# Keys and values of linear attention packed in 64-row halves: the summary product on four array quarters

## The chip, the cores and the metric

The kernel runs on one core of one Trainium2 chip. What counts is the device time of one execution in microseconds. The core has a matrix engine (TensorE, in the profile PE, with its weight loads as a row of their own, PEld), a vector engine (VectorE, DVE), an activation engine (ScalarE, ACT), GpSimd (POOL) and the engine SyncE (SP), which here only issues DMAs.

## The reference, cut to what matters

```python
def _attn_ref(q, k, v):                      # 8 batches, 8 heads, 576 positions, 64 wide
    q_s = np.exp(q - np.max(q, axis=-1, keepdims=True))
    q_s = q_s / (np.sum(q_s, axis=-1, keepdims=True) + 1e-09)
    k_s = np.exp(k - np.max(k, axis=2, keepdims=True))          # over the 576 positions
    k_s = k_s / (np.sum(k_s, axis=2, keepdims=True) + 1e-09)
    kv = np.einsum('bhsd,bhse->bhde', k_s, v)                   # a 64x64 summary of each head
    return np.einsum('bhsd,bhde->bhse', q_s, kv)
```

Behind it come two blocks on the 4608 rows of 512 columns: a gated causal convolution (`val = x @ w_val`, a gate of five taps, `@ w_out`), and a channel mix (`k = relu(xk @ w_k)`, `v = k*k @ w_v`, `r = sigmoid(xr @ w_r)`, result `r * v`). All of it is in fp32. The large products are made of three products of rounded halves (`passes`, line 576); the small ones of the attention are plain fp32 matmuls, each of which shows in the profile as two weight loads and two MATMUL records.

## The kernel before, in words

The rows are taken in 12 blocks of 384 (`main_steps`), each through the products V (`pv`), Y (`py`), R (`racc`), H (`ph`) and A (`vacc`). Beside them runs the attention. Its keys and values are taken in 16 *rounds* of four heads (`rounds`, two for each batch). A round has these steps: load (`k_load`, `v_load`), the maximum of the keys over the positions (`kv_max`, then either `kv_turn` through TensorE or `later_top` through VectorE and two DMAs), subtract and exponential (`kv_exp` or `later_kexp`), and the summary product with its division (`kv_mm`).

In `kv_max` to `kv_mm` before, the 576 positions of a head lie on 128 partitions as four full slices and a fifth slice of 64 rows; the other 64 rows of that slice are filled with -3.0e38 for the keys and with zeros for the values, by GpSimd (lines 298 and 315). Two loads fetch the keys of a round, five its values. The maximum is four elementwise maxima of 128x256 (lines 341 and 344). The product (line 419) has 20 matmuls in a round: two pairs of heads, five slices, and in each pair one head on either half of the array's columns, all 128 rows contracted. The values carry a column of ones, so that column 64 of the product is the sum to divide by. The product lies in one PSUM bank `kvacc`.

For batch 0 the summaries go into `kvf`, a block-diagonal tile, and `kv_spread` (line 443) copies them into `kvc`, from which `x_cross` (line 630, blocks 1 and 2) and `x_quads` (line 646, blocks 3 to 11) multiply the queries, four 64x64 quarters at a time.

The order of the work: the first two blocks, the decoding of the 64-bit weights and rounds 0 to 4 come in the hand-written list `FRONT`; from block 2 on steps follow `main_steps`, with the side work put behind step numbers by `REST` (`mm0` behind step 6, `quads` behind 14, `mm1` behind 20). A planner then orders each engine's instructions by its own costs; `after(...)` and `issue_after` pin single instructions behind others. PSUM has three pools: `ps_acc` with 3 banks, `ps_w` with 3 and `ps_t` with 2. The small tiles of the attention (`pmT`, `mx`, `pq`, `kvacc`, half of `px`) come from `ps_t`.

Of the kernel before, what the change touches and what calls it, by code (L numbers as in the profile page):

```python
# [8 lines left out]
F32 = mybir.dt.float32  # L9
# [66 lines left out]
def tile_linear_attention_gated_conv_channel_mix(  # L76
# [15 lines left out]
    nc = tc.nc  # L92
# [198 lines left out]
    LEAST = -3.0e38  # L291
# [3 lines left out]
    def frame(vt):  # L295
        nc.gpsimd.memset(vt[:, :, 0:NS4, D:VW], 1.0)
        nc.gpsimd.memset(vt[:TAIL, :, NS4, D:VW], 1.0)
        nc.gpsimd.memset(vt[TAIL:P, :, NS4, :], 0.0)

    vt = odd.tile([P, HR, NST, VW], F32, name="vt")  # L300
    kt1 = first.tile([P, HR, NST, D], F32, name="kt1")
    vt1 = first.tile([P, HR, NST, VW], F32, name="vt1")
    frame(vt)
    frame(vt1)

    def k_load(st):
        b, j = st["at"]
        src = k[b, HR * j:HR * (j + 1)]
        t = st["k"] = kt1 if st is rounds[1] else work.tile([P, HR, NST, D], F32, tag="kt", bufs=1, name="kt")
        nc.sync.dma_start(  # L310
            t[:, :, 0:NS4, :].rearrange("p h s d -> p h (s d)"),
            src[:, 0:KT, :].rearrange("h (p s) d -> p h (s d)", s=NS4),
        )
        nc.sync.dma_start(t[:TAIL, :, NS4, :], src[:, KT:S, :].rearrange("h p d -> p h d"))
        nc.gpsimd.memset(t[TAIL:P, :, NS4, :], LEAST)

    def v_load(st):
        b, j = st["at"]
        src = v[b, HR * j:HR * (j + 1)]
        t = st["v"] = vt1 if st is rounds[1] else vt  # L320
        if b == 0:
            st["dense"] = early.tile([P, HR, NS4, D], F32, tag="raw", bufs=6, name="dense")
            nc.sync.dma_start(
                st["dense"].rearrange("p h s d -> p h (s d)"), src[:, 0:KT, :].rearrange("h (p s) d -> p h (s d)", s=NS4)
            )
        else:
            for h in range(HR):
                nc.sync.dma_start(t[:, h, 0:NS4, 0:D], src[h, 0:KT, :].rearrange("(p s) d -> p s d", s=NS4))
        nc.sync.dma_start(t[:TAIL, :, NS4, 0:D], src[:, KT:S, :].rearrange("h p d -> p h d"))

    def v_copy(st):
        with after("xf.0" if st is rounds[1] else "shifted"):
            nc.scalar.copy(st["v"][:, :, 0:NS4, 0:D], st["dense"])

    def kv_max(st):
        kt = st["k"]
        whole_pm = scratch("pm")
        pm = whole_pm[:, 0:HR * D]
        one = pm.rearrange("p (h d) -> p h d", d=D)
# [5 lines left out]
        st["pm"] = whole_pm  # L345
# [6 lines left out]
    def kv_turn(st):  # L352
        pm, n, x = st["pm"], HR * D // P, rounds.index(st)
        pmT = bank_of(st, "pmT", 1)
        with after((None, "heat", "matmul", "matmul")[x] if x < 4 else "matmul"):
            for j in range(n):
                nc.tensor.transpose(pmT[:, j * P:(j + 1) * P], pm[:, j * P:(j + 1) * P], f32(ident))
        m1 = odd.tile([P, n], F32, tag="m1", bufs=2, name="m1")
        with after("kvf.0" if x == 1 else None):
            latest[f"m1.{x}"] = nc.vector.tensor_reduce(  # L360
                out=m1, in_=pmT[:, :n * P].rearrange("p (j t) -> p j t", j=n), axis=AX.X, op=ALU.max
            )
        st["m1"] = m1
# [6 lines left out]
    def later_top(st, ring, width):  # L370

        t, G = st["pm"], HR * D // SQ
        nc.vector.transpose(out=t[:, 0:HR * D], in_=t[:, 0:HR * D])
        four = t[:, HR * D:HR * D + NA * G].rearrange("p (a g) -> p a g", a=NA)
        nc.vector.tensor_reduce(
            out=four[:, 0], in_=t[:, 0:HR * D].rearrange("p (g y) -> p g y", g=G), axis=AX.X, op=ALU.max
        )
        for a in range(1, NA):
            nc.vector.tensor_copy(four[0:SQ, a], four[a * SQ:(a + 1) * SQ, 0])
        nc.vector.tensor_reduce(  # L380
            out=t[0:SQ, 0:G], in_=four[0:SQ].rearrange("p a g -> p g a"), axis=AX.X, op=ALU.max
        )
        nc.vector.transpose(out=t[0:SQ, 0:SQ], in_=t[0:SQ, 0:SQ])
        line = turns.tile([G, SQ], F32, tag="line", bufs=2, name="line")
        nc.sync.dma_start(line, t[0:G, 0:SQ])
        every = st["every"] = work.tile([P, width], F32, tag=ring[0], bufs=ring[1], name="every")[:, 0:HR * D]
        nc.sync.dma_start(every, line.rearrange("(o g) x -> o (g x)", o=1).to_broadcast([P, HR * D]))

    def later_kexp(st, behind):
        kt = st["k"]  # L390
        with tc.issue_after(behind.ins):
            latest["less"] = nc.vector.tensor_sub(
                kt, kt, st["every"].rearrange("p (h o d) -> p h o d", o=1, d=D).to_broadcast([P, HR, NST, D])
            )
        latest["kexp"] = nc.scalar.activation(kt, kt, AF.Exp)

    def kv_exp(st):

        kt, m1, n = st["k"], st["m1"], HR * D // P
# [9 lines left out]
    def kv_mm(st):  # L409

        b, j = st["at"]
        kt, n = st["k"], HR // 2
        acc = bank_of(st, "kvacc", 0)
        head = lambda x, e: 2 * x + (e ^ x & 1 if b else e)
        for x in range(n):
            for s in range(NST):
                for e in range(2):
                    with after("heat" if st is rounds[0] and x + s + e == 0 else None):
# [9 lines left out]
        if b == 0:
            for e in range(2):
                p = slice(e * D, (e + 1) * D)  # L430
                latest[f"kvf.{j}"] = nc.vector.tensor_mul(
                    kvf[p, n * j:n * (j + 1), p], sums[p, :, 0:D], d3[p].to_broadcast([D, n, D])
                )
            return
        nc.vector.tensor_mul(kvc[b % 2][:, n * j:n * (j + 1), :], sums[:, :, 0:D], d3.to_broadcast([P, n, D]))
# [596 lines left out]
```

## Time and profile before

| | |
|---|---|
| median of three runs | 785.2 us (784.32 to 785.59) |
| the profiled execution | 784.37 us |
| its span, first to last instruction | 782.6 us |
| TensorE (PE) busy | 769.3 us, 98% |
| weight loads (PEld) busy | 668.9 us, 85% |
| VectorE (DVE) busy | 562.3 us, 72% |
| ScalarE (ACT) busy | 463.2 us, 59% |
| granted TensorE clock | 0.999 |

The time of an execution is the span and 1.77 us around it. Busy times overlap; the engine whose time adds up to the end is read from the chain of work that ended last and from the stages.

### The profile page before, as it was taken

The numbers are of one execution on the slowest core, as the hardware profiler recorded it, in microseconds if no ns is written. First come the engines' busy times: TensorE is split into PE (matmuls) and PEld (weight loads), VectorE is DVE, ScalarE is ACT, GpSimd is POOL, SyncE is SP. The second block draws the span as 40 slices with busy tenths as digits, with TensorE's granted clock in tenths as the row PEclk, the third lists the DMA queues.
The fourth block names the chain that finished last, engine by engine and source line by source line (L and its number), as shares of the span: only waits on it lengthen the run. The fifth ranks groups of instructions, "written<-read, shape, count | busy, mean of one in ns | idle before, by whom it ended". The sixth has DMA issues, their size and how long they took to land.

```text
span 782.6 us, 12491 instructions
## 1 busy us (share of the span) xinstructions
PE 769.3 (98%) x4498; PEld 668.9 (85%) x4498; DVE 562.3 (72%) x1121; ACT 463.2 (59%) x926; POOL 67.7 (9%) x221
## 2 busy tenths in 40 slices
PE   6999999999999999999999999999999999999998
PEld 5545688899899989889889899989989999989996
DVE  6999999679778578578678587686877856753611
ACT  5787948636735745744763763763673673573542
POOL 1020012000101101000010110200010110100000
PEclk9999999999999999999999999999999999999999
DMA  9887320135133303302431411511523211101001
GB/s 316 263 281 217 75 67 1 41 105 145 48 102 103 87 22 98 111 1 82 136 82 67 123 41 48 142 41 48 142 53 98 74 54 42 60 21 41 2 1 40
DMA packets 91708, 68.88 MB, mean 88 GB/s; under 512 B 48738, under 2 KB 83454, under 8 KB 91646
## 3 DMA queue, kind: packets, MB, share of 16 engines
q1 hardware_dynamic: 91600, 68.06, 29.1%
q8 instruction: 35, 0.57, 0.3%
q14 instruction: 27, 0.22, 0.1%
q10 hardware_dynamic: 46, 0.02, 0.0%
HBM read 51.54 MB, written 16.53 MB: 87 GB/s over the span
## 4 chain that ended last, share of the span: by engine, by line
PE 87%; ACT 3%; DVE 1%; issue 0%
PE vacc L576 24%; PE ph L576 23%; PE py L576 12%; PE pv L576 12%; PE racc L576 11%; PE kvacc L419 2%; PE px L646 2%; ACT wk_hi L271 0%; PE px L630 0%; ACT wv_hi L271 0%; ACT wr_hi L271 0%; ACT q L619 0%; DVE qt L499 0%; DVE qs L495 0%; ACT wout_hi L271 0%; PE pq L603 0%
## 5 line engine op out<-in xcount | busy, mean ns | idle before, releaser
L569 DVE TENSOR_TENSOR kl<-rf,kh 128x384 fp32r<-128x384 f32 x88 | 48.9, 555 | 142.0 <-ACT kh L568 142.0
L576 PE MATMUL ph<-xkl,wk_hi 128*128 128x384 f32 x352 | 118.2, 336 | 0.0
L576 PE MATMUL ph<-xkh,wk_hi 128*128 128x384 f32 x352 | 118.2, 336 | 0.0
L576 PE MATMUL ph<-xkh,lower 128*128 128x384 f32 x352 | 118.2, 336 | 0.0
L722 DVE SCALAR_TENSOR_TENSOR gate<-xf,cw,gate 128x384 f32<-128x384 f32 x192 | 108.9, 611 | 3.2 <-ACT gate L719 2.7
L576 PE MATMUL vacc<-wv_hi,kh 128*128 128x512 f32 x276 | 109.9, 398 | 0.0
L576 PE MATMUL vacc<-wv_hi,kl 128*128 128x512 f32 x276 | 107.7, 391 | 0.0
L840 ACT ACTIVATE rf<-ph 128x384 f32<-128x384 f32 x96 | 47.1, 491 | 101.1 <-PE ph L576 101.0
L568 ACT CAST gh<-gf 128x384 fp32r<-128x384 f32 x44 | 22.6, 514 | 113.6 <-DVE gf L774 113.6
L576 PEld LDWEIGHTS ph<-xkh,wk_hi 128*128 128x128 f32 x352 | 66.1, 188 | 2.6
L576 PEld LDWEIGHTS ph<-xkh,lower 128*128 128x128 f32 x352 | 66.1, 188 | 2.6
L576 PEld LDWEIGHTS ph<-xkl,wk_hi 128*128 128x128 f32 x352 | 66.1, 188 | 0.0
L576 PEld LDWEIGHTS vacc<-wv_hi,kh 128*128 128x128 f32 x276 | 51.8, 188 | 15.3 <-issue 6.2
L813 DVE SCALAR_TENSOR_TENSOR xm<-yf,mus,xm 128x384 f32<-128x384 f32 x96 | 55.3, 610 | 12.4 <-ACT xm L812 12.3
L576 PEld LDWEIGHTS vacc<-wv_hi,kl 128*128 128x128 f32 x276 | 51.7, 188 | 11.3 <-DVE kl L569 0.3
L576 PE MATMUL py<-gh,wout_hi 128*128 128x384 f32 x176 | 60.1, 341 | 0.0
L576 PE MATMUL py<-gl,wout_hi 128*128 128x384 f32 x176 | 59.1, 337 | 0.0
L576 PE MATMUL pv<-xl,wval_hi 128*128 128x384 f32 x176 | 58.9, 335 | 0.0
L576 PE MATMUL py<-gh,lower 128*128 128x384 f32 x176 | 58.9, 336 | 0.0
L576 PE MATMUL pv<-xh,wval_hi 128*128 128x384 f32 x176 | 58.9, 335 | 0.0
L576 PE MATMUL pv<-xh,lower 128*128 128x384 f32 x176 | 58.9, 334 | 0.0
L576 PE MATMUL vacc<-wv_lo,kh 128*128 128x512 f32 x144 | 56.2, 390 | 0.0
(149 smaller groups left out, 1632.7 us busy)
## 6 DMA issues: line engine op xcount, KB each, us to landing
out_dram<-rs SPq DMA_DIRECT2D x36, 256.0 KB, 2.1
kt<-in_k_dram SPq DMA_DIRECT2D x16, 512.0 KB, 4.8
vt<-in_v_dram SPq DMA_DIRECT2D x56, 128.0 KB, 3.7
turned<-sq SPq DMA_DIRECT2D x36, 192.0 KB, 2.7
qT<-turned SPq DMA_DIRECT2D x72, 96.0 KB, 2.2
qn<-in_q_dram SPq DMA_DIRECT2D x24, 192.0 KB, 3.5
raw<-in_moe_w_k_dram SPq DMA_DIRECT2D x8, 512.0 KB, 5.4
raw<-in_moe_w_v_dram SPq DMA_DIRECT2D x8, 512.0 KB, 4.5
```

The lines of the kernel that those rows point to most:

```text
L419: nc.tensor.matmul(acc[e * D:(e + 1) * D, x * VW:(x + 1) * VW], lhsT=kt[:, head(x, e), s, :], rhs=st["v"][:, head(x, e), s, :], start=(s = ...
L568: latest["round"] = nc.scalar.copy(pair[0], a)
L569: latest["split"] = nc.vector.tensor_sub(pair[1], a, f32(pair[0]))
L576: latest["matmul"] = nc.tensor.matmul(po, lhsT=left[a], rhs=right[b], start=start and x == 0, stop=stop and x == len(m) - 1)
L646: latest["matmul"] = nc.tensor.matmul(st["px", c][cols, o:o + n].rearrange("p (a y) -> p a y", y=w), lhsT=kvc[b % 2][rows, c, :], rhs=st[" ...
L722: latest[f"tap.{sh}"] = nc.vector.scalar_tensor_tensor(out=gx(gate), in0=xv[:, :, HALO - sh:HALO - sh + L], scalar=tap(c, HALO - sh), in1= ...
L813: latest["mix"] = nc.vector.scalar_tensor_tensor(out=gx(xf), in0=yv[:, :, 1:], scalar=mu[:, c:c + 1], in1=gx(xf), op0=ALU.mult, op1=ALU.add)
L840: nc.scalar.activation(rf, ph[:, :T], AF.Relu)
```

## The change

Positions are laid out as 64 partitions of nine slices instead of 128 of four and a half, and two heads of different parity stand one above the other: rows 0 to 63 hold the even heads of a round, rows 64 to 127 the odd ones. There is no padding. The fifth slice, its fillers and their loads go. One load fetches the keys of a round, two its values (in batch 0 still a dense load, a small one and a copy by ScalarE).

`kv_max` is one `tensor_reduce` over a strided view. What it leaves is 128 columns wide instead of 256, so `kv_turn` has one transpose instead of two and `later_top` works on half the columns; `every` comes back in two DMAs of 64 partitions. `kv_exp` spreads the maxima with two matmuls on the halves of the columns instead of two transposes.

`kv_mm` has 36 matmuls of 64 rows by 64 columns instead of 20 of 128 by 64: nine slices, two head pairs, two halves. Each row half writes to a PSUM bank of its own. The division has two additions and two scalar multiplies of 128x64 where there was one of each; in batch 0 half of the multiplies go to ScalarE. `kv_spread` is pinned behind round 3's subtraction and exponential. In `FRONT`, `spread` stands behind `mm3`, `xturn3.1 xq3.1` stand ahead of `wv7 swv7 H7.0`, and `cross0.2 x0.2 gate0.2` behind `A0.1`.

```diff
-    "qexp.1 spread turn3 exp3 A2.0 wv3 H5.0 lwv7 lwv5 mm3 qnorm.1 xturn0.1 xq0.1 wv5 swv5 A3.0 wv6 swv6 xturn1.1 "
-    "xq1.1 H6.0 cross0.1 x0.1 gate0.1 A4.0 x1.1 xturn2.1 xq2.1 wv7 swv7 H7.0 swval0 xturn3.1 xq3.1 gate1.1 A5.0 "
+    "lwv4 H1.0 H2.0 wk4 lwv6 wv0 mm2 wk5 rsig.0 A0.0 lwv3 H3.0 wk6 wv4 swv4 max3 A1.0 wk7 H4.0 wv2 qexp.1 turn3 exp3 "
+    "A2.0 wv3 H5.0 lwv7 lwv5 mm3 spread qnorm.1 xturn0.1 xq0.1 wv5 swv5 A3.0 wv6 swv6 xturn1.1 xq1.1 H6.0 cross0.1 "
+    "x0.1 gate0.1 A4.0 x1.1 xturn2.1 xq2.1 xturn3.1 xq3.1 wv7 swv7 H7.0 swval0 gate1.1 A5.0 cross1.1 x2.1 x3.1 swval1 "
...
+    def heads(st, a):
+        b, j = st["at"]
+        return a[b, HR * j:HR * (j + 1)].rearrange("(g x) (p s) d -> (x p) g s d", x=2, s=NS)
...
-            nc.vector.tensor_max(one, kt[:, :, 0, :], kt[:, :, 1, :])
-        for x in range(2, NST):
-            with after("qmul" if st is rounds[1] and x > 2 else None):
-                nc.vector.tensor_max(one, one, kt[:, :, x, :])
+            nc.vector.tensor_reduce(
+                out=pm[:, 0:P].rearrange("p (g d) -> p g d", g=NG), in_=st["k"].rearrange("p g s d -> p g d s"),
+                axis=AX.X, op=ALU.max,
+            )
...
-            for j in range(n):
-                nc.tensor.transpose(mx[:, j * P:(j + 1) * P], m1[:, j:j + 1].to_broadcast([P, P]), f32(ident))
+            for n, half in enumerate(HALVES):
+                nc.tensor.matmul(
+                    mx[half, 0:P], lhsT=m1[:, n:n + 1].to_broadcast([P, D]), rhs=f32(ident), start=True, stop=True
+                )
...
-        acc = bank_of(st, "kvacc", 0)
-        head = lambda x, e: 2 * x + (e ^ x & 1 if b else e)
-        for x in range(n):
-            for s in range(NST):
-                for e in range(2):
+        acc = [bank_of(st, "kvacc", 0) for _ in range(2)]
+        for s in range(NS):
+            for g in range(NG):
+                for x, half in enumerate(HALVES):
...
-                            acc[e * D:(e + 1) * D, x * VW:(x + 1) * VW], lhsT=kt[:, head(x, e), s, :],
-                            rhs=st["v"][:, head(x, e), s, :], start=(s == 0), stop=(s == NST - 1),
+                            acc[x][HALVES[x ^ g], 0:VW], lhsT=st["k"][half, g, s, :], rhs=st["v"][half, g, s, :],
+                            start=(s == 0), stop=(s == NS - 1),
...
+        for x in range(2):
+            nc.vector.tensor_scalar_add(den[:, x:x + 1], acc[x][:, D:VW], EPS)
         nc.vector.reciprocal(den, den)
...
+                if g:
+                    nc.scalar.activation(to, acc[x][here, 0:D], AF.Copy, scale=den[here, x:x + 1])
...
+                with after("sub.3" if g else "kexp.3"):
+                    move(kvc[0][HALVES[x ^ g], x:NC:NG, :], kvf[half, g:NC:NG, half])
```

## Rows read from the trace of the kernel before

**Rows 1.** Page, part 1: busy time of each engine, share, instructions.

```profile
PE 769.3 (98%) x4498; PEld 668.9 (85%) x4498; DVE 562.3 (72%) x1121; ACT 463.2 (59%) x926; POOL 67.7 (9%) x221
```

**Rows 2.** Windows: length, PE, PEld, DVE, ACT, POOL busy (instructions), PEclk, DMA share, GB/s.

```profile
28.00:60.00 32.00, 31.41 (x92) 16.52 (x91) 30.26 (x62) 25.49 (x50) 6.30 (x17) 1.00 0.86 266
60.00:100.00 40.00, 38.73 (x224) 22.59 (x223) 37.99 (x69) 35.53 (x69) 2.47 (x5) 1.00 0.52 147
170.00:782.00 612.00, 609.03 (x3622) 552.67 (x3620) 414.25 (x845) 341.43 (x693) 47.09 (x150) 1.00 0.24 70
```

**Rows 3.** Page, part 4: the chain that ended last, by line.

```profile
PE vacc L576 24%; PE ph L576 23%; PE py L576 12%; PE pv L576 12%; PE racc L576 11%; PE kvacc L419 2%; PE px L646 2%; ACT wk_hi L271 0%; PE px L630 0%; ACT wv_hi L271 0%; ACT wr_hi L271 0%; ACT q L619 0%; DVE qt L499 0%; DVE qs L495 0%; ACT wout_hi L271 0%; PE pq L603 0%
```

**Rows 4.** Waits of PE: us in total, times, longest.

```profile
PE kvacc L419 <- ACT kt L407: 1.8, 1, 1.8
...
PE px L630 <- ACT q L619: 0.9, 1, 0.9
...
PE pq L603 <- DVE qt L499: 0.5, 1, 0.5
```

**Rows 5.** Timeline of PE around one round's product: start, length, instructions.

```profile
614.53 0.34 PE L576 MATMUL py<-gl,wout_hi 128*128 128x384 f32 x1
614.80 1.39 PE L419 MATMUL kvacc<-vt,kt 128*64 128x65 f32 x40
616.11 0.44 PE L576 MATMUL py<-gh,wout_hi 128*128 128x384 f32 x1
```

**Rows 6.** Timeline of PE around one `x_quads`.

```profile
200.63 1.52 PE L646 MATMUL px<-qT,kvc 64*64 64x384 f32 x16
202.08 0.50 PE L576 MATMUL vacc<-wv_hi,kh 128*128 128x512 f32 x1
```

**Rows 7.** Windows of 20 ns in that `x_quads`: PE, PEld, ACT busy (instructions running).

```profile
200.62:200.64 0.02, 0.01 (x2) 0.01 (x2) 0.00 (x0) 1.00 0.45 103
200.64:200.66 0.02, 0.02 (x4) 0.02 (x4) 0.00 (x0) 1.00 0.00 0
...
201.00:201.02 0.02, 0.02 (x7) 0.01 (x3) 0.00 (x0) 1.00 0.00 0
...
201.32:201.34 0.02, 0.02 (x7) 0.01 (x2) 0.00 (x0) 1.00 0.00 0
```

**Rows 8.** Operations of VectorE by line: ns min/median/max, first and last start, forms.

```profile
L344 DVE TENSOR_TENSOR pm<-pm,kt x48: 407/417/439, 7.0 to 601.0; 128x256 f32<-128x256 f32 x48
...
L375 DVE TENSOR_REDUCE pm<-pm x11: 419/420/421, 171.2 to 601.9; 128x8 f32<-128x256 f32 x11
...
L404 DVE TENSOR_TENSOR kt<-kt,mx x5: 1472/1480/1501, 10.9 to 117.3; 128x1280 f32<-128x1280 f32 x5
...
L426 DVE TENSOR_SCALAR den<-kvacc x16: 141/151/166, 15.5 to 616.5; 128x2 f32<-128x2 f32 x16
L431 DVE TENSOR_TENSOR kvf<-kvacc,den x4: 220/289/295, 16.2 to 24.6; 64x128 f32<-64x128 f32 x4
...
L520 DVE TENSOR_REDUCE qm<-qn x18: 931/946/954, 150.1 to 650.1; 128x12 f32<-128x768 f32 x18
```

**Rows 9.** Timeline of VectorE at the start of the kernel.

```profile
6.14 0.95 DVE L484 TENSOR_REDUCE qm<-came 128x12 f32<-128x768 f32 x1
7.00 0.41 DVE L344 TENSOR_TENSOR pm<-pm,kt 128x256 f32<-128x256 f32 x1
```

**Rows 10.** Timeline of ScalarE: the copies of `kv_spread`.

```profile
25.33 0.60 ACT L443 COPY kvc<-kvf 64x128 f32<-64x128 f32 x2
```

**Rows 11.** Waits between 28 and 100 us, VectorE on a load of weights.

```profile
DVE raw L176 <- DMA raw<-in_moe_w_k_dram: 1.1, 1, 1.1
```

**Rows 12.** Timeline of PE: the two transposes of the maximum in round 1.

```profile
16.92 0.38 PE L357 MATMUL pmT<-ident,pm 128*128 128x128 f32 x2
```

**Rows 13.** Timeline of ScalarE: the exponential of round 5.

```profile
179.85 1.28 ACT L395 ACTIVATE kt<-kt 128x1280 f32<-128x1280 f32 x1 [2.08 <-DVE kt L392]
```

**Rows 14.** Chain in order of time: round 5's product.

```profile
182.69 1.32 PE kvacc L419 x40
```

More of the change, by code (lines that the diff above doesn't have):

```diff
@@ L286, in tile_linear_attention_gated_conv_channel_mix @@
     nc.gpsimd.memset(kvf, 0.0)
-    LEAST = -3.0e38
+    HALVES = slice(0, D), slice(D, P)
     SQ = 32
     NA = P // SQ
[L295 to L304, printed above, removed]
@@ L306, in k_load, with v_tile @@
-    def k_load(st):
[L307 to L315, printed above, removed]
+    def v_tile(pool, name):
+        t = pool.tile([P, NG * NS * VW + 2], F32, name=name)[:, 0:NG * NS * VW].rearrange("p (g s c) -> p g s c", g=NG, s=NS)
+        nc.gpsimd.memset(t[:, :, :, D:VW], 1.0)
+        return t
@@ new lines, in tile_linear_attention_gated_conv_channel_mix @@
+    vt = v_tile(odd, "vt")
+    kt1 = first.tile([P, NG, NS, D], F32, name="kt1")
+    vt1 = v_tile(first, "vt1")
+    def heads(st, a):
+        b, j = st["at"]
+        return a[b, HR * j:HR * (j + 1)].rearrange("(g x) (p s) d -> (x p) g s d", x=2, s=NS)
+    def k_load(st):
+        t = st["k"] = kt1 if st is rounds[1] else work.tile([P, NG, NS, D], F32, tag="kt", bufs=1, name="kt")
+        nc.sync.dma_start(t.rearrange("p g s d -> p g (s d)"), heads(st, k).rearrange("p g s d -> p g (s d)"))
@@ L317, in v_load @@
     def v_load(st):
         b, j = st["at"]
-        src = v[b, HR * j:HR * (j + 1)]
+        src = heads(st, v)
         t = st["v"] = vt1 if st is rounds[1] else vt
[L321 to L328, printed above, removed]
@@ L329, in v_load @@
-        nc.sync.dma_start(t[:TAIL, :, NS4, 0:D], src[:, KT:S, :].rearrange("h p d -> p h d"))
+        if b:
+            for g in range(NG):
+                nc.sync.dma_start(t[:, g, :, 0:D], src[:, g])
+            return
+        st["dense"] = early.tile([P, NG, NS1, D], F32, tag="raw", bufs=6, name="dense")
+        nc.sync.dma_start(
+            st["dense"].rearrange("p g s d -> p g (s d)"), src[:, :, 0:NS1, :].rearrange("p g s d -> p g (s d)")
+        )
+        nc.sync.dma_start(t[:, :, NS1, 0:D], src[:, :, NS1, :])
@@ L331, in v_copy @@
     def v_copy(st):
         with after("xf.0" if st is rounds[1] else "shifted"):
-            nc.scalar.copy(st["v"][:, :, 0:NS4, 0:D], st["dense"])
+            nc.scalar.copy(st["v"][:, :, 0:NS1, 0:D], st["dense"])
     def kv_max(st):
[L336 to L339, printed above, removed]
+        pm = st["pm"] = scratch("pm")
         with after({1: "m1.0", 2: "gf.3", 3: "sub.2"}.get(rounds.index(st))):
-            nc.vector.tensor_max(one, kt[:, :, 0, :], kt[:, :, 1, :])
@@ L370, in later_top @@
     def later_top(st, ring, width):
-        t, G = st["pm"], HR * D // SQ
-        nc.vector.transpose(out=t[:, 0:HR * D], in_=t[:, 0:HR * D])
-        four = t[:, HR * D:HR * D + NA * G].rearrange("p (a g) -> p a g", a=NA)
+        t, G = st["pm"], P // SQ
+        nc.vector.transpose(out=t[:, 0:P], in_=t[:, 0:P])
+        four = t[:, P:P + NA * G].rearrange("p (a g) -> p a g", a=NA)
         nc.vector.tensor_reduce(
-            out=four[:, 0], in_=t[:, 0:HR * D].rearrange("p (g y) -> p g y", g=G), axis=AX.X, op=ALU.max
+            out=four[:, 0], in_=t[:, 0:P].rearrange("p (g y) -> p g y", g=G), axis=AX.X, op=ALU.max
         )
@@ L380, in later_top @@
         nc.vector.tensor_reduce(
-            out=t[0:SQ, 0:G], in_=four[0:SQ].rearrange("p a g -> p g a"), axis=AX.X, op=ALU.max
+            out=t[0:SQ, 0:2 * G].rearrange("p (x g) -> p x g", x=2),
+            in_=four[0:SQ].rearrange("p (x a) g -> p x g a", x=2), axis=AX.X, op=ALU.max,
         )
         nc.vector.transpose(out=t[0:SQ, 0:SQ], in_=t[0:SQ, 0:SQ])
[L384 to L387, printed above, removed]
+        line = turns.tile([2 * G, SQ], F32, tag="line", bufs=2, name="line")
+        nc.sync.dma_start(line, t[0:2 * G, 0:SQ])
+        every = st["every"] = work.tile([P, width], F32, tag=ring[0], bufs=ring[1], name="every")[:, 0:P]
+        for x, half in enumerate(HALVES):
+            nc.sync.dma_start(
+                every[half], line[x * G:(x + 1) * G].rearrange("(o g) y -> o (g y)", o=1).to_broadcast([D, P])
+            )
     def later_kexp(st, behind):
@@ L392, in later_kexp @@
             latest["less"] = nc.vector.tensor_sub(
-                kt, kt, st["every"].rearrange("p (h o d) -> p h o d", o=1, d=D).to_broadcast([P, HR, NST, D])
+                kt, kt, st["every"].rearrange("p (g o d) -> p g o d", o=1, d=D).to_broadcast([P, NG, NS, D])
             )
@@ L411, in kv_mm @@
         b, j = st["at"]
-        kt, n = st["k"], HR // 2
-        acc = bank_of(st, "kvacc", 0)
-        head = lambda x, e: 2 * x + (e ^ x & 1 if b else e)
-        for x in range(n):
-            for s in range(NST):
-                for e in range(2):
-                    with after("heat" if st is rounds[0] and x + s + e == 0 else None):
+        acc = [bank_of(st, "kvacc", 0) for _ in range(2)]
+        for s in range(NS):
+            for g in range(NG):
+                for x, half in enumerate(HALVES):
+                    with after("heat" if st is rounds[0] and x + s + g == 0 else None):
@@ L427, in kv_mm @@
+                            start=(s == 0), stop=(s == NS - 1),
+                        )
+        den = odd.tile([P, 2], F32, tag="den", bufs=2, name="den")
+        for x in range(2):
+            nc.vector.tensor_scalar_add(den[:, x:x + 1], acc[x][:, D:VW], EPS)
         nc.vector.reciprocal(den, den)
[L428 to L434, printed above, removed]
@@ L435, in kv_mm @@
-        nc.vector.tensor_mul(kvc[b % 2][:, n * j:n * (j + 1), :], sums[:, :, 0:D], d3.to_broadcast([P, n, D]))
-    def kv_spread():
-        for e in range(2):
-            for odd_one in range(2):
-                here, there = (slice(x * D, (x + 1) * D) for x in (e, e ^ odd_one))
-                move = nc.vector.tensor_copy if odd_one else nc.scalar.copy
-                move(kvc[0][there, odd_one:NC:2, :], kvf[here, odd_one:NC:2, here])
+        for x, half in enumerate(HALVES):
+            if b:
+                nc.vector.tensor_scalar_mul(out=kvc[b % 2][:, NG * j + x, :], in0=acc[x][:, 0:D], scalar1=den[:, x:x + 1])
+                continue
+            for g in range(NG):
+                here, to = HALVES[x ^ g], kvf[half, NG * j + g, half]
+                if g:
+                    nc.scalar.activation(to, acc[x][here, 0:D], AF.Copy, scale=den[here, x:x + 1])
+                else:
+                    latest[f"kvf.{j}"] = nc.vector.tensor_scalar_mul(
+                        out=to, in0=acc[x][here, 0:D], scalar1=den[here, x:x + 1]
+                    )
@@ L445, in segments, with summary @@
+    def kv_spread():
+        for x, half in enumerate(HALVES):
+            for g in range(NG):
+                move = nc.vector.tensor_copy if g else nc.scalar.copy
+                with after("sub.3" if g else "kexp.3"):
+                    move(kvc[0][HALVES[x ^ g], x:NC:NG, :], kvf[half, g:NC:NG, half])
+    def summary(b, c, e):
+        return kvc[b % 2][HALVES[e], c // NG * NG + (e ^ c & 1), :]
     def segments(i):
@@ L630, in x_cross @@
                     latest["matmul"] = nc.tensor.matmul(
-                        st["px", c][cols, at], lhsT=kvc[b % 2][rows, c, :], rhs=st["q", c][rows, at], start=True, stop=True
+                        st["px", c][cols, at], lhsT=summary(b, c, e), rhs=st["q", c][rows, at], start=True, stop=True
                     )
@@ L647, in x_quads @@
                             st["px", c][cols, o:o + n].rearrange("p (a y) -> p a y", y=w),
-                            lhsT=kvc[b % 2][rows, c, :], rhs=st["qT"][rows, c // 2, at, c % 2, :], start=True, stop=True,
+                            lhsT=summary(b, c, e), rhs=st["qT"][rows, c // 2, at, c % 2, :], start=True, stop=True,
                         )
```

27 lines of the change are left out of this document (10 added, 17 removed), and 23 rows, old and new, of the table FRONT.

## The prediction

> **What bounds the kernel now.** I read the busy times first: TensorE works 98% of the span, VectorE 72%, ScalarE 59% [rows 1]. The chain that ended last says the same by line: it is nearly all matmuls, and the summary product (`kvacc`) holds 2% of it [rows 3]. An average can hide stages, so the windows come next. From 170 to 782 us TensorE is busy 609.03 of 612 us, while VectorE has 414 and ScalarE 341: work taken from those two is worth nothing there, and work taken from TensorE is worth its full length [rows 2]. Before 100 us it is different: VectorE is busy 38.0 of 40 us and ScalarE 35.5 between 60 and 100 us, the DMA engines 86% of the time between 28 and 60 us, and TensorE still shows gaps [rows 2]. The waits of TensorE name them: 1.8 us for the first exponential of the keys, 0.9 us for a copy of queries by ScalarE, 0.5 us for the normalized queries [rows 4]. So there are two accounts: TensorE's own time in all rounds, and the waits of the first 100 us.
>
> **The product on quarters.** A round's product takes 1.31 us, from 614.80 to the next matmul at 616.11 [rows 5]. How much of this is the price of changing the shape of the array is read from `x_quads`: 16 records take 1.45 us to the next matmul [rows 6], in groups of four that begin 0.32 us apart (201.00, 201.32) [rows 7]. Four groups are 1.28 us; 0.17 us is left for getting in and out. With the same 0.17 us, the 40 records of a round, two at a time, have 20 slots of (1.31 - 0.17) / 20 = 0.057 us. After the change there are 36 matmuls, 72 records. If four run at once, they need 18 slots: 18 x 0.057 + 0.17 = 1.20 us, 0.11 us less. That is the removed padding (576 rows in place of 640), not more: the old form already ran two at once on full height, so four at half height are the same rate.
>
> Do four run at once? `x_quads` goes over the same four quarters in the same order, each matmul as two records. Within its first 40 ns four records run, and at 201.00 three more begin within 20 ns [rows 7]. So I take 18 slots. The other bound is two at a time: 36 slots, 36 x 0.057 + 0.17 = 2.22 us, 0.91 us more. Rounds 2 to 15 lie where TensorE is full, so this term is 14 x -0.114 = -1.6 us, with +12.7 us as its far end. The point at which the term turns is a slot of 1.14 / 18 = 0.063 us.
>
> The Trainium skill (TensorE: Matmul & The Clock Gate, section "Wait — 56ns, not 53.3ns?") says that matmuls never start less than about 25 ns apart, however small they are. The start of three records within 20 ns disagrees with it [rows 7], but there the records are long and few. By that rule 72 records would need at least an estimated 1.8 us.
>
> The transposes: one of two in `kv_turn` goes, at most 0.19 us (two take 0.38) [rows 12]; the two matmuls that spread the maximum change the array's shape and back, at most the 0.17 us above. I take zero for the pair; only rounds 2 to 4 count, so the ends are -0.6 and +0.5 us.
>
> **VectorE.** Back to back, 0.09 us of an operation overlaps the next (a reduce of 0.95 us at 6.14 is followed at 7.00) [rows 9]. Four maxima of 0.417 us are 4 x 0.33 = 1.31 us. A reduce costs 0.420 us for 256 columns and 0.946 for 768 [rows 8], 1.03 ns a column, so 1152 columns are 1.34, or 1.25 us behind another: 0.06 less. No row shows a reduce whose neighbours lie 256 bytes apart; it may cost as much as twice that, +1.25 us a round, and it can hardly cost less than the dense one. I take the dense price, since a maximum is one pass over the same columns in either form.
>
> The Trainium skill (VectorE: DVE Perf Modes, "Rules for kernel authors") calls `tensor_reduce` the slowest VectorE operation and advises to restructure it, which speaks against this edit. The rows have 0.420 us for a reduce and 0.417 for a maximum of 256 columns: at fp32 they are equal [rows 8].
>
> The subtraction loses 128 of 1280 columns. Its slope is (1480 - 417) / 1024 = 1.04 ns a column [rows 8]: -0.13 us. The reduce over the turned maximum loses half of 256 columns: -0.13. The two multiplies into `kvf` lose 64 columns each: -0.13 together, and two more go to ScalarE. A second addition for the divisor costs 0.151 - 0.09 = +0.06 [rows 8]. A round of batch 0 is 0.06 + 0.13 + 0.13 + 0.13 - 0.06 = 0.39 us shorter on VectorE, the two rounds 0.8 us. They lie ahead of the first large products, where TensorE waits for exactly this chain [rows 4]. But behind them the loads of weights are close to their limit, and VectorE itself waits 1.1 us for one [rows 2, 11], so what comes earlier may wait there. Between 0 and -0.8 I take -0.4 us.
>
> From round 5 on VectorE's savings are worth nothing [rows 2]. The longer way to `every` (a second DMA to issue) is covered: the exponential of round 5 ends at 181.13, its product begins at 182.69, 1.56 us later [rows 13, 14], and the edits take four shorter operations out of the same path. The two banks of `ps_t` that a product now takes at once are read out by VectorE some microseconds later; the next `quads` is eight steps on. Were this cover gone, each late microsecond in a round would be one of TensorE.
>
> **ScalarE and the order.** `kv_spread` ran at 25 us [rows 10]; it now comes behind round 3's exponential, in the stretch where ScalarE is busy 89% [rows 2], and its two copies cost 0.6 us there. Against that, `xq3.1` moves ahead of a weight's decoding and splitting, and it is the copy of queries for which TensorE waited 0.9 us [rows 4]. Between -0.9 and +0.6 I take -0.3 us. A key exponential shorter by a tenth (1.28 us at 1280 columns [rows 13]) goes into that.
>
> **The sum.** -1.6 - 0.4 - 0.3 = -2.3 us. The profiled execution took 784.37 us, so 782.1 on its account. The median of the runs lies 0.8 us above that execution; on the median's account the forecast is 785.2 - 2.3 = 782.9 us.
>
> **The rivals.**
>
> - The gain is absorbed: the loads set the first 100 us and ScalarE's extra copies meet the saved wait, while a slot of four records costs 0.061 us instead of 0.057. For it speaks the DMA share of 0.86 [rows 2]. Then -14 x 0.04 = -0.6 us is left: 784.6 us.
> - The strided reduce takes double. Rounds 0 to 2 run where VectorE is full or waited for: 3 x 1.25 = +3.75 us, with -1.6 from TensorE 787.3 us. Against it: nothing in the rows makes a column of a reduce dearer than 1.03 ns, but all of them are dense.
> - Slower, on the other side: the quarters run only two at a time, because both records of a matmul go to the same quarter and the second holds back those behind it. Then it is +12.7 - 0.7 = +12.0 us, 797.2 us. Against it speaks `x_quads` [rows 7]. The whole becomes slower than noise from a slot of about 0.072 us: 14 x (18 x 0.015) is 3.8 us, against 2.3 of gain.
> - TensorE can't take records faster than some rate. Before, 40 came in 1.31 us, 33 ns apiece, and no row shows a longer stretch of faster ones [rows 5]. If records had to start 27 ns apart, 72 would take 1.94 + 0.17 us, +0.8 a round, 795.7 us with the gains of the start. The Trainium skill's 25 ns (same section as above) are this rival's rule; by it the estimate is 794.
>
> **How the numbers follow.** Forecast 0.60, absorbed 0.18, strided reduce 0.07, two at a time 0.09, record rate 0.06. A measurement here tells about 0.2% from no change, 1.6 us. So faster is 0.60, within it 0.18, slower 0.22. The forecast's own range runs from 781.3 (all of -1.6, -0.8, -0.9 and -0.6) to 783.6. The range reaches from 780.4 (0.9 us lower, as far as the lowest run before lay below the median) to 787.5: it takes in the absorbed gain and the strided reduce and leaves out the last two rivals, 0.15.
>
> **What would show it.** After the change, the product should take 1.20 us from its first record to the next matmul, with four records in each slot; 2.2 would be two at a time, anything from 1.8 the rate. The single reduce of 1152 columns should read 1.34 us; 2.5 is the strided price. The first division, which began at 15.5 us [rows 8], should come some tenths earlier, the wait for `q` before `px` should be gone, and TensorE busy from 170 us on should lose about 1.3 us. The prediction is wrong if the product doesn't shorten, or if the front, ordered anew, puts a wait where there was none.

## The result, and the profile after

The change makes the kernel slower: 791.91 us (median of 6 runs, 790.29 to 794.22) against 785.02 us (6 runs, 784.11 to 785.59), a ratio of 1.0093 with an interval of 1.0076 to 1.0111. That is 7 us where 2.3 us of gain were forecast, and above the range. The profiled execution took 790.29 us, its span is 788.5.

TensorE's total hardly differs from before, VectorE's is 7.7 us longer [rows 1]; page, part 1, of after:

```profile
PE 770.0 (98%) x5015; PEld 667.3 (85%) x5015; DVE 570.0 (72%) x1103; ACT 464.4 (59%) x930; POOL 65.4 (8%) x201
```

The product does what was forecast. Timeline of TensorE around the round that [rows 5] shows:

```profile
620.41 0.34 PE L574 MATMUL py<-gl,wout_hi 128*128 128x384 f32 x1
620.68 1.28 PE L411 MATMUL kvacc<-vt,kt 64*64 64x65 f32 x72
621.89 0.44 PE L574 MATMUL py<-gh,wout_hi 128*128 128x384 f32 x1
```

From its start to the next matmul are 1.21 us, 0.10 less than before. The maximum does not. The groups of VectorE in after (count | busy, mean ns of one | idle ahead of it):

```profile
L332 DVE TENSOR_REDUCE pm<-kt 128x128 f32<-128x1152 f32 x16 | 35.2, 2203 | 2.6 <-DMA kt<-in_k_dram 2.6
L384 DVE TENSOR_TENSOR kt<-kt,every 128x1152 f32<-128x1152 f32 x11 | 14.9, 1352 | 0.0
```

The reduce takes 2.20 us (in the median 2.24), not 1.34; the subtraction over just as many columns takes 1.35. Where the time went is seen in the windows (columns as in [rows 2]), here of after:

```profile
12.00:14.00 2.00, 2.00 (x76) 1.83 (x78) 2.00 (x2) 1.97 (x3) 0.00 (x0) 1.00 1.05 394
14.00:28.00 14.00, 10.74 (x133) 6.80 (x126) 12.58 (x29) 9.13 (x17) 0.82 (x6) 1.00 0.86 295
28.00:60.00 32.00, 31.75 (x96) 16.37 (x96) 30.50 (x57) 25.09 (x49) 5.95 (x17) 1.00 0.84 264
60.00:100.00 40.00, 36.06 (x266) 20.48 (x265) 38.73 (x68) 36.34 (x71) 1.16 (x2) 1.00 0.42 131
100.00:168.00 68.00, 65.94 (x384) 57.26 (x385) 55.15 (x90) 42.46 (x85) 9.57 (x17) 0.97 0.11 33
170.00:787.00 617.00, 614.85 (x4007) 557.74 (x4005) 423.83 (x851) 342.16 (x696) 46.23 (x140) 1.00 0.24 70
```

and of before in the stretches that [rows 2] leave out:

```profile
12.00:14.00 2.00, 0.16 (x5) 0.16 (x6) 2.00 (x5) 1.48 (x2) 0.00 (x0) 1.00 1.15 364
14.00:28.00 14.00, 13.13 (x127) 8.98 (x126) 13.12 (x29) 10.72 (x20) 1.13 (x7) 1.00 0.90 329
100.00:168.00 68.00, 68.00 (x391) 60.07 (x390) 56.58 (x103) 43.37 (x87) 7.79 (x18) 1.00 0.15 42
```

TensorE's idle time (length less busy) between 12 and 168 us is 1.84 + 0.87 + 0.59 + 1.27 + 0 = 4.6 us before and 0 + 3.26 + 0.25 + 3.94 + 2.06 = 9.5 us after. The third block's first V product begins at 167.95 us before and 174.95 after, and between 168 us and there TensorE is never idle in after. From the third block to the end of the span it is 614.65 us before and 613.55 after. So everything from there on is 1.1 us faster, where about 1.3 were forecast, and the front loses 7.0 us: 4.9 us of it are more idle time, and 2.1 us are longer busy time, of which a lower clock makes about 1.4 (below). The waits of TensorE up to 130 us, in after:

```profile
PE mx L395 <- DVE m L349: 3.0, 1, 3.0
PE pmT L346 <- DVE pm L332: 2.5, 2, 2.1
...
PE pq L601 <- DVE qt L497: 1.9, 1, 1.9
PE pq L601 <- ACT kvf L426: 1.3, 1, 1.3
PE pq L601 <- PE vacc L574: 1.0, 1, 1.0
```

In [rows 4] the longest were 1.8, 0.9 and 0.5. The wait for the first exponential is gone (the first product begins at 13.01 us, before at 13.84), as is the one of 0.9 us for `q`, and five others stand in their place: for the maximum (`pm`, `m`), for the queries (`qt`), and for the banks of `ps_t`, in which `pq` can begin only when the product of the round has been read out (`kvf` at 27 us; the third, at 90 us, is put down to `vacc`, which ended where the wait began, while VectorE came to read `kvacc` out only at 90.39 us). The wait for `qt` shows the reduce at work: VectorE runs that of round 1 from 12.63 to 14.83 us, ahead of the reciprocal and the multiply that `qt` needs, and so the first division comes at 16.08 us and not, as forecast, earlier than 15.5. One of the waits costs more than its length; timeline of TensorE in after around the maximum of round 4:

```profile
114.68 0.33 PE L574 MATMUL pv<-xl,wval_hi 128*128 128x384 f32 x1
114.85 0.34 PE L574 MATMUL pv<-xh,wval_hi 128*128 128x384 f32 x1
117.25 0.44 PE L346 MATMUL pmT<-ident,pm 128*128 128x128 f32 x1 [2.06 <-DVE pm L332]
...
118.13 0.52 PE L574 MATMUL pv<-xh,wval_hi 128*128 128x384 f32 x1
118.45 0.52 PE L574 MATMUL pv<-xh,lower 128*128 128x384 f32 x1
```

Ahead of the wait the matmuls began 0.17 us apart, after it 0.32. The granted clock (third column from the end) says why:

```profile
114.00:116.00 2.00, 1.19 (x7) 0.87 (x6) 2.00 (x4) 1.03 (x2) 0.19 (x1) 1.00 0.00 0
116.00:118.00 2.00, 0.75 (x3) 0.76 (x4) 2.00 (x3) 0.00 (x0) 0.00 (x0) 0.83 0.00 0
118.00:120.00 2.00, 2.00 (x9) 1.56 (x9) 1.00 (x4) 0.60 (x2) 0.00 (x0) 0.50 0.00 0
120.00:122.00 2.00, 2.00 (x12) 1.67 (x13) 1.75 (x3) 0.44 (x2) 0.00 (x0) 0.82 0.01 4
```

TensorE had waited 2.06 us and then ran at half its clock, 1.2 GHz: (1 - 0.50) x 2 + (1 - 0.82) x 2 = 1.4 us more. It is not the length of the wait alone: the one of 1.9 us for `qt`, at 14 to 16 us, and the one of 3.0 us for `m`, at 78 to 81 us, left the clock at 1.00. The profiled execution is the shortest of the six, with a mean clock of 0.998; the two longest, 793.39 and 794.22 us, had 0.993, so the clock takes more from the median than from this trace.

### The profile page after: what moved, and what is told of

Read it like the earlier page. It is cut to its first block, busy times and chain, and to the rows that moved or that the text cites. A ratio compares the mean times of both kernels' runs of the same rounds, so it can differ in the third digit from the quotient of the medians.

```text
span 788.5 us, 13426 instructions
## 1 busy us (share of the span) xinstructions
PE 770.0 (98%) x5015; PEld 667.3 (85%) x5015; DVE 570.0 (72%) x1103; ACT 464.4 (59%) x930; POOL 65.4 (8%) x201
## 4 chain that ended last, share of the span: by engine, by line
PE 90%; DVE 5%; DMA 2%; ACT 1%; issue 1%; SPq 0%; ACTq 0%; DVEq 0%
PE vacc L574 25%; PE ph L574 24%; PE py L574 13%; PE pv L574 11%; PE racc L574 11%; PE kvacc L411 2%; PE px L644 2%; DMA kt<-in_k_dram 1%; DVE pm L332 1%; DMA raw<-in_moe_w_k_dram 1%; PE pq L601 1%; DVE gate L720 1%; DVE whole L176 1%; PE px L628 0%; DVE qt L497 0%
```

## The experiments

Theories after the result. **A**: the reduce is dear because its neighbours lie 256 bytes apart, and the front pays for it. **B**: the two banks and the division in more pieces hold `ps_t` longer. **C**: the new order (`FRONT`, pins) is worse. **D**: the product costs something that its own length doesn't show. Ratios are to the kernel before on the same chip.

**The maximum.** e1 is after with the maximum as five elementwise maxima, of which three in round 1 are pinned behind `qmul` (two before, none in after). e8 keeps the one reduce, but over nine neighbouring elements, so that it takes maxima of other elements than the reference's. e2 is before with one reduce over slices.

```diff
 e1
-            nc.vector.tensor_reduce(out=pm[...], in_=st["k"].rearrange("p g s d -> p g d s"), ...)
+            nc.vector.tensor_max(two, kt[:, :, 0:2, :], kt[:, :, 2:4, :])
+        for x in (4, 6):
+                nc.vector.tensor_max(two, two, kt[:, :, x:x + 2, :])
+        nc.vector.tensor_max(one, two[:, :, 0, :], two[:, :, 1, :])
+            nc.vector.tensor_max(pm[...], one, kt[:, :, NS1, :])
 e8
+                in_=st["k"].rearrange("p g s d -> p g (s d)").rearrange("p g (d s) -> p g d s", s=NS),
 e2 (before)
+            nc.vector.tensor_reduce(out=one, in_=kt.rearrange("p h s d -> p h d s"), axis=AX.X, op=ALU.max)
```

> The changed kernel with its one strided reduce of 1152 columns replaced by five elementwise maxima whose neighbours are contiguous (three of 256 columns, two of 128). Strided-reduce theory (each reduce takes 2.09 to 2.24 us instead of 1.25, and as one piece it blocks VectorE in the first 125 us): most of the 7 us goes, 783 to 786 us, the waits of TensorE for the maximum (3.0 and 2.5 us) fall under 1 us together. Bank theory (a product now holds both banks of ps_t until VectorE has read them, and the transposes of the queries wait) or order theory (the new FRONT list and the pins of spread): no more than 2 us gained, 788 to 791 us, the waits of pq before the queries' transposes stay.

> The changed kernel with its single reduce over groups of nine neighbouring elements instead of nine elements 256 bytes apart; it takes the maximum over other elements than the reference's, and nothing else changes. If the stride is what makes the reduce dear, it reads about 1.34 us instead of 2.24 and the kernel comes to 786 to 789 us, near the run with dense elementwise maxima (788.7). If a reduce of 1152 columns into 128 is dear in itself, it stays at 2.1 to 2.2 us and the kernel at 790 to 793 us.

> The kernel before with nothing changed but the maximum: one strided reduce of 1280 columns in place of four maxima of 256. Strided-reduce theory: the reduce reads about 2.4 us against 1.3 us for the four maxima, five times in the front, so +4 to +7 us, 789 to 792 us. Bank or order theory: within 1.5 us of before.

Measured: e1 788.73 us, 1.0053 (1.0037 to 1.0069); e8 788.24 us, 1.0039 (1.0024 to 1.0055); e2 789.75 us, 1.0072 (1.0048 to 1.0097). The reduce itself by line, of e8 and of e2:

```profile
L332 DVE TENSOR_REDUCE pm<-kt 128x128 f32<-128x1152 f32 x16 | 21.5, 1346 | 2.7 <-DMA kt<-in_k_dram 2.7
```

```profile
L341 DVE TENSOR_REDUCE pm<-kt 128x256 f32<-128x1280 f32 x16 | 38.9, 2433 | 3.3 <-DMA kt<-in_k_dram 3.3
```

The same instruction over as many columns takes 1.35 us with neighbours side by side and 2.20 with neighbours 256 bytes apart. A holds: dense maxima give back (1.0093 - 1.0053) x 784.5 = 3.1 us, the dense reduce of e8 4.2 us, and the strided one alone, put into before (e2), costs 5.6 us. But more than half of the loss remains in e1, which is less than A alone let expect: its waits for the maximum are still 1.7 us (`pm`) and 1.1 us (`m`).

**Banks and order.** e3 is before with two banks and the split division, e4 is before with the new `FRONT` and pins. e5 is e1 with the old `FRONT` and no pins; e6 is e1 with all multiplies into `kvf` on VectorE; e7 is e5 and e6 together.

```diff
 e3 (before)
+        acc = [bank_of(st, "kvacc", 0) for _ in range(n)]
+        for x in range(n):
+            nc.vector.tensor_scalar_add(den[:, x:x + 1], acc[x][:, D:VW], EPS)
 e4 (before): FRONT of after, and
+                with after("sub.3" if odd_one else "kexp.3"):
 e6 (e1)
-                if g:
-                    nc.scalar.activation(to, acc[x][here, 0:D], AF.Copy, scale=den[here, x:x + 1])
```

> The kernel before with the product's two head pairs in two PSUM banks and the division split as in the changed kernel, layout, maximum, order and matmuls as before. Bank theory: the transposes of the queries wait for the second bank, +2 to +3 us, 787 to 788 us. Strided-reduce and order theory: 785 us within 1 us.

> The kernel before with the changed kernel's FRONT list and with its kv_spread pinned behind round 3, nothing else. Order theory: over 2 us slower, 787 us or more. Strided-reduce and bank theory: 785 us within 1.5 us.

> Dense elementwise maxima as in the earlier run (788.7 us), and the FRONT list of the kernel before, without the pins on kv_spread. Order theory (the new list and pins don't fit the shortened operations): at least 2 us faster, 786.5 us or less. Theory that the rest sits in the two banks and the division, with ScalarE's half of it: within 1 us of 788.7.

> Dense elementwise maxima, the new order, and in batch 0 all four multiplies into kvf on VectorE, none on ScalarE. Division theory (the transposes of the queries wait for both banks, which ScalarE reads last, 1.3 us at 27 us and 0.7 at 17): 1 to 2 us faster than 788.7, 786.5 to 787.7. Order theory: within 0.8 us of 788.7.

> Both of the last two together: dense maxima, the old order, kvf on VectorE alone. What stays changed is the 64-row layout, its loads and the product on quarters with its two banks. If all of the loss is in the maximum, the order and ScalarE's half of the division, this is faster than the kernel before by the 0.11 us a round on TensorE: 782.5 to 784 us. If the two banks and the layout themselves cost, 785 to 787.5 us.

Measured: e3 786.17 us, 1.0018 (1.0008 to 1.0027); e4 783.95, 0.9991 (0.9982 to 1.0001); e5 789.53, 1.0067 (1.0052 to 1.0082); e6 787.95, 1.0045 (1.003 to 1.006); e7 788.37, 1.0051 (1.0036 to 1.0066). C falls: the new order by itself loses nothing (that it gains a little is not clear of noise), and the old one with the new form is no better. ScalarE's half of the division makes no difference clear of noise either (e6 against e1, e7 against e5), and e7 lies above both of its ranges. The two banks and the split division (B) cost 1.4 us alone, less than forecast, and by what way is not shown: e3's trace has no wait of TensorE for a bank. The waits that grew are those for `qt`, from 0.5 to 1.1 us, and for `m`, from 0.3 to 0.5. The granted clock was 0.88, 0.50 and 0.77 in the three slices from 14 to 20 us, (0.12 + 0.50 + 0.23) x 2 = 1.7 us, behind the wait of 1.8 us for the first exponential, behind which it stayed at 1.00 before.

**One wait at a time.** In e6 the `pmT` at 17 us waits for `kvf` and the `pq` at 90 us for a bank; the maximum of round 3 comes late. e9 takes `pmT` of round 1 and the second bank of rounds 2 to 4 from `ps_w`. e10 pins the queries' work on VectorE behind round 1's division and round 3's maximum. e11 does both.

```diff
 e9 (e6)
+        pmT = ps_w.tile([P, 512], F32, tag="w", name="pmT") if x == 1 else bank_of(st, "pmT", 1)
+        acc.append(ps_w.tile([P, 512], F32, tag="w", name="kvacc") if st in rounds[2:5] else bank_of(st, "kvacc", 0))
 e10 (e6)
+        with after("sub.0" if h.stop == HR else "top.3" if "top.3" in latest and "m1.4" not in latest else None):
+        with after("split" if "m1.4" in latest else "kvf.1" if h.start else None):
```

> e6 (dense maxima, all divisions of batch 0 on VectorE) with the banks alone changed: the second accumulator of rounds 2 to 4 and the turned maximum of round 1 come from ps_w, so that TensorE's next small transposes need not wait until VectorE has read a bank out. VectorE's order stays that of e6. If the banks are behind what is left (e6 is 3.5 us slower than before), the wait of 0.7 us of pmT for kvf at 17 us and that of 1.1 us of pq at 90 us go, and the time falls by 1.1 to 1.8 us against e6, to a ratio of 1.0025 to 1.003. If only VectorE's order counts, the two waits turn into others and the time stays within 0.4 us of e6 (1.004 to 1.005).

> e6 with VectorE's order alone changed: the normalizing multiply of the second half of block 0's queries is pinned behind the division of round 1, and the sum of block 1's queries behind the maximum of round 3. If VectorE's order is behind the rest, the wait of pq for kvf at 27 us shrinks from 1.3 to about 0.8 us and that of pmT for the maximum of round 3 at 79 us (1.8 us) goes: 2.0 to 2.4 us less than e6, ratio 1.0015 to 1.002. If only the banks count, at most 0.5 us is gained (ratio 1.004).

> Both edits together. If banks and order are two separate causes, they add up: 3 to 4 us less than e6, the time of the kernel before or up to 0.5 us below it (ratio 0.9993 to 1.0007). If they are one and the same stall seen twice, it is the better of the two alone. If something else holds the front (loads of weights), nothing below 1.003 comes out.

Measured: e9 788.4 us, 1.0057 (1.0042 to 1.0072); e10 788.72, 1.0062 (1.0047 to 1.0077); e11 788.13, 1.0059 (1.0042 to 1.0075). None gained on e6. e9 and e10 lie above all that was expected, though within the noise of e6's 1.0045; e11 fits its last alternative, that something else holds the front. The waits named did change, but others grew. TensorE's idle time from 14 us to the third block is 6.85 us in e6, 6.89 in e9, 5.73 in e10, and in e10 the granted clock is 0.50 between 80 and 82 us, behind a wait of 2.4 us for `pm`.

**Which rounds.** Now the new form (with dense maxima and two banks) was put into some rounds only, the others left as before: from round 5 on (e12, and e13 with the new `FRONT` and pins), from round 2 (e14), from round 4 (e18).

```diff
+    def packed(st):
+        return rounds.index(st) >= FROM
+    def k_load(st):
+        if packed(st):
+            return k_packed(st)
+    def summary(b, c, e):
+        slot = c // NG * NG + (e ^ c & 1) if NR * b + c // NG >= FROM else c
+        return kvc[b % 2][HALVES[e], slot, :]
```

> Rounds 0 to 4 in every respect as in the kernel before (128-row layout, one bank, four maxima, old list); from round 5 on the 64-row halves, the product on quarters, two banks and dense maxima. If the whole loss sits in the rounds of the first 170 us and the later rounds only gain, the time is 11 x 0.11 = 1.2 us below the kernel before: ratio 0.998 to 0.999, and the third block begins within 0.3 us of before. If the later rounds lose something too (two banks of ps_t held until VectorE reads them, the second load of the maxima), the ratio is 1.000 or more.

> The same with the new list FRONT and the pinned kv_spread, which alone gave a ratio of 0.9991. If the two gains add up, 1.6 us below the kernel before (ratio 0.9975 to 0.9985), the fastest of all. If the order's gain was chance, the time of the run without it.

> Rounds 0 and 1 as before, rounds 2 and later in the new form with dense maxima and two banks, old list. Of the dense form's loss (4 us, and TensorE idle for 7.0 us in place of 2.7 between 14 us and the third block) this leaves out what happens in the two rounds of batch 0. If the divisions of batch 0 and what follows them before 30 us are the main part (TensorE idle there 2.3 us in place of 0.9), the ratio is 0.999 to 1.001. If the rounds of batches 1 and 2 lose as much through their banks and late maxima, 1.002 to 1.004.

> Rounds 0 to 3 as before, rounds 4 and later in the new form, old list. If the loss is in rounds 2 and 3, which run beside the decoding of the weights, the time is that of the version with the new form from round 5 on (ratio 0.998 to 0.999). If round 4 loses as much as the others, about a third of the loss is there: 0.9995 to 1.0005.

Measured: e12 783.2 us, 0.9978 (0.9967 to 0.9988); e13 782.5 us, 0.9972 (0.9963 to 0.9981); e14 787.27 us, 1.0032 (1.0021 to 1.0044); e18 782.96 us, 0.9977 (0.9968 to 0.9985). D falls: where the new form doesn't touch the front it gains. e13 beats both kernels, the one before by 2.2 us. And rounds 2 and 3 alone make the difference between e18 and e14, 4.3 us.

**Rounds 2 and 3.** e15 is e14 with the second bank from `ps_w`, e16 is e14 with the pin behind round 3's maximum, e17 has both, the new `FRONT` and pins.

```diff
 e15 (e14)
+        pool, tag = (ps_w, "w") if st in rounds[2:5] else (ps_t, "t")
 e16 (e14)
+        with after("sub.0" if h.stop == HR else "top.3" if "top.3" in latest and "m1.4" not in latest else None):
```

> The run with rounds 2 and later in the new form, its second accumulator of rounds 2 to 4 taken from ps_w instead of ps_t. If the bank that the product holds is a cause, the wait of 1.06 us of pq at 90 us goes and the time falls by 0.8 to 1.1 us (ratio 1.0018 to 1.0022). If the removed wait only moves, it stays at 1.003.

> The same run with VectorE's order changed at one place: the sum of block 1's queries comes behind the maximum of round 3. If the late maximum is a cause, the wait of 1.60 us of pmT at 78 us shrinks to under 0.5 us and the time falls by 1.1 to 1.6 us (ratio 1.001 to 1.002). If the queries are then the late ones, it stays at 1.003.

> Both, with the new list FRONT and the pinned kv_spread. If bank, late maximum and order are separate causes, 2.2 to 3 us come back and the ratio is 0.9995 to 1.0005; if they share one limit (the loads of weights and VectorE together), 1.002 or more.

Measured: e15 788.56 us, 1.0045 (1.0033 to 1.0058); e16 787.4, 1.0036 (1.0024 to 1.0049); e17 787.79, 1.0036 (1.0022 to 1.0049). Again the waits moved. In e15 the bank's wait at 90 us is gone, and a wait for a copy of queries, 0.6 us in e14, is 1.9 us, with the lower clock behind it:

```profile
102.53 0.89 PE L727 MATMUL px<-q,kvc 64*64 64x192 f32 x10 [1.93 <-ACT q L716]
```

```profile
104.00:106.00 2.00, 2.00 (x6) 1.59 (x5) 2.00 (x5) 2.00 (x5) 2.00 (x1) 0.50 0.02 4
```

So the limit is not in the wait that TensorE shows last. e18 and e14 differ in rounds 2 and 3 alone. On VectorE their traces part at the maximum of round 2, at 43 us. (The DMA queues differ before: e14 issues two loads of `w_v` in a row at 37.90 us and then three of `w_k`, e18 one of `w_v`, one of `w_k` and again one of `w_v`.) VectorE there in e18, then in e14:

```profile
44.16 1.82 DVE L908 SCALAR_TENSOR_TENSOR xm<-yf,mus,xm 128x384 f32<-128x384 f32 x3
46.21 1.15 DVE L908 SCALAR_TENSOR_TENSOR xm<-yf,mus,xm 128x384 f32<-128x384 f32 x2 [0.24 <-ACT xm L907]
47.28 0.77 DVE L180 TENSOR_SCALAR raw<-raw 128x512 uint32<-128x512 uint32 x2
47.96 1.89 DVE L181 SCALAR_TENSOR_TENSOR whole<-raw 128x512 uint32<-128x512 uint32 x3
```

```profile
44.81 1.15 DVE L908 SCALAR_TENSOR_TENSOR xm<-yf,mus,xm 128x384 f32<-128x384 f32 x2
47.59 0.43 DVE L180 TENSOR_SCALAR raw<-raw 128x512 uint32<-128x512 uint32 x1 [1.62 <-DMA raw<-in_moe_w_k_dram]
47.93 1.14 DVE L908 SCALAR_TENSOR_TENSOR xm<-yf,mus,xm 128x384 f32<-128x384 f32 x2
48.99 0.77 DVE L180 TENSOR_SCALAR raw<-raw 128x512 uint32<-128x512 uint32 x2
49.68 1.88 DVE L181 SCALAR_TENSOR_TENSOR whole<-raw 128x512 uint32<-128x512 uint32 x3
```

The planned order of e14 has a decoding (line 180) ahead of two mixes (`xm`) which in e18 run ahead of it. Its weight has not come, and VectorE stands still for 1.62 us. The decoding that frees three buffers of weights (line 181) begins 1.7 us later, and so do the loads that wait for these buffers. Timeline of the DMA queue in e18, then in e14:

```profile
48.67 1.53 SPq L245 DMA_DIRECT2D raw<-in_moe_w_k_dram  x3
```

```profile
50.38 1.53 SPq L245 DMA_DIRECT2D raw<-in_moe_w_k_dram  x3
```

The windows from 50 to 55 us of e18 and of e14 show a DMA share of 0.96 and of 0.62:

```profile
50.00:55.00 5.00, 5.00 (x13) 2.23 (x12) 3.82 (x10) 3.04 (x6) 3.38 (x6) 1.00 0.96 315
```

```profile
50.00:55.00 5.00, 5.00 (x13) 2.10 (x12) 5.00 (x11) 3.05 (x6) 2.72 (x3) 1.00 0.62 195
```

and from 28 to 100 us ScalarE waits 0.4 us for loads of `w_k` in e18 and 4.0 in e14:

```profile
ACT raw L174 <- DMA raw<-in_moe_w_k_dram: 0.4, 1, 0.4
```

```profile
ACT raw L174 <- DMA raw<-in_moe_w_k_dram: 4.0, 2, 2.1
```

TensorE's own waits in that stretch are 0.9 + 0.6 = 1.5 us in e18 and 2.0 + 1.6 + 1.1 + 0.4 = 5.1 us in e14. e15 and e16 have the decoding at the same place and stand still there for 0.97 and 1.83 us. That the late loads are the cause is read from these traces and not shown: no run moved that one decoding back. A low DMA share alone doesn't cost the time, since e13, the fastest, has 0.70 between 50 and 55 us. Nor are the loads the only limit: in e11 (1.0059) VectorE and ScalarE wait 1.6 us in all for weights between 28 and 100 us, as much as in the kernel before. Which edit of rounds 2 and 3 brought the planner to the other order stays open.

## Why the prediction was wrong

The steps that hold form a row of runs, each one edit from the next:

| edit | runs | us |
|---|---|---|
| new form, dense maxima, in rounds 4 to 15 | before to e18 | -1.8 |
| in rounds 2 and 3 too | e18 to e14 | +4.3 |
| in batch 0 too | e14 to e5 | +2.7 |
| new list and pins | e5 to e1 | -1.1 |
| one strided reduce for the maxima | e1 to after | +3.1 |

Each is the difference of two ratios times 784.5 us. By the intervals of the ratios the first is uncertain by 0.7 us and the others by 1.1 to 1.9 us, so that the step of the list and pins is not clear of noise; the sum is 7.2, and 1.0093 is 7.3. The shares hold for this sequence only: the strided reduce costs 5.6 us where it comes first (e2) and 3.1 where it comes last. Nor is batch 0's step one of waits alone: in e5's trace the clock is 0.65 and 0.50 in the two slices from 82 to 86 us, behind a wait of 2.8 us for `pm`, (0.35 + 0.50) x 2 = 1.7 us, while e14's is at 1.00 there.

- **The product** was right in mechanism and size: 1.21 us where 1.20 was forecast. Four run at once, so "two at a time" falls. The rate of records doesn't bind either: 72 in 1.21 us are 17 ns apiece, where before had 33. The Trainium skill's floor of about 25 ns between starts (TensorE: Matmul & The Clock Gate, "Wait — 56ns, not 53.3ns?") does not agree with this.
- **"I take the dense price, since a maximum is one pass over the same columns in either form"** failed. The price is 2.24 us, between the two ends that were set (1.34 and twice that). It was a rival at 0.07, and its 787.3 counted the reduce in rounds 0 to 2 by its own length; the run with the reduce alone (e2) lost 5.6 us (1.0072), and the two longest waits in after (3.0 and 2.06 us) belong to the maxima of rounds 3 and 4, which the rival left out. The Trainium skill has the rule that was missed (SBUF — State Buffer, "Door 1: The DMA port swizzle", the note on cachelines): a new 16-byte line costs extra, so that an fp32 operand can't step far for free. The measured 2.20 against 1.35 us agrees in sign; no run here tried other steps.
- **"Between 0 and -0.8 I take -0.4 us"** for VectorE in the front, and "between -0.9 and +0.6" for ScalarE and the order, failed most: 4.3 + 2.7 - 1.1 = 5.9 us (by the intervals uncertain by about 2) came in place of -0.7, without the reduce. The working added up the lengths of the instructions that got shorter. It did not ask where a planner puts them when their lengths change, though between 28 and 100 us VectorE, the buffers of weights and the loads hang on each other. The clock was at nothing in the sum, though the new waits lowered it (1.4 us in after). The last sentence of the prediction named "a wait where there was none", but gave it no chance and no price. In which rounds the loss arises is shown by the runs; the way from the edits to the late instructions is read from traces and stays open.
- **"The two banks ... the next `quads` is eight steps on"** stands in a paragraph on the rounds from 5 on and was right for these, as e12 shows. For the front the banks were put at nothing, though transposes of queries (`pq`) soon follow there and wait 1.1 us in e14. It is only one link: taking the bank away moved the wait. The Trainium skill (TensorEngine Tiling (Array Packing), "Gotcha 1: PSUM Pressure") says that row tiling raises the pressure on PSUM and that different row tiles write to different banks. The waits for a bank in after, 1.3 and 1.0 us, agree.
- **From round 5 on VectorE's time is worth nothing** was right: after's last 613.55 us are shorter by the product's gain although each reduce there is 0.9 us too long. e12, e13, e14 and e18 have 613.5 to 613.8 us there.
- The forecast of 782.9 us is the time of e13 (782.5): the gain of the product, perhaps with the order's, and none of the front's loss. That the two agree to 0.4 us is chance, since e13 has no shorter VectorE work in the front, which the forecast counted.

## What to carry to other kernels

A new layout that is good for the steady rounds need not be put into the start: there, where several engines and the loads hang on each other, price an edit by what it delays and not by its length, and keep the form that the order was fitted to. When a wait that was removed comes back elsewhere, compare two runs that differ in as few rounds as possible and look for the first instruction that begins later, not for the longest wait. Here a maximum over an axis that isn't the innermost was cheaper as elementwise maxima over dense rows than as one strided reduce (e1 against after, before against e2).

## What the runs showed of the hardware

- A `tensor_reduce` of 1152 fp32 columns took 2.20 us with neighbours 256 bytes apart and 1.35 us side by side: 1.9 and 1.2 ns a column.
- 72 records on four quarters went by in 1.21 us, 17 ns apiece.
- Behind some waits of 1.8 to 2.8 us TensorE was granted 0.50 of its clock in one of the next 2 us slices of the profile (after at 118 us, e3 at 16, e5 at 84, e10 at 80, e15 at 104), but it stayed at 1.00 behind waits of 1.9 and 3.0 us in after and of 1.8 us before. Where it fell it cost, by an estimate from the clock of each slice, 1.4 us (after) and, with 0.50 and 0.65 in two slices of e10, 1.7 us, about 0.7 of the wait.
